# Attention and two feed-forward layers on one core: the first units in halves, means of V in column groups, masks over half the rows

## The chip, the cores and the metric

One core of a Trainium2 chip runs the whole program. The metric is the device time of one execution in microseconds; the median of several runs stands for a kernel, and the profile shows one more execution, recorded instruction by instruction.

## What is computed

The reference chains three parts over 2 batches of 768 tokens (8 heads of 64, so 512 features):

```python
# attention: each query sees keys closer than 16 and one summary per block of 32
k_sum = k.reshape(B, H, nb, 32, D).max(axis=3)
v_sum = v.reshape(B, H, nb, 32, D).mean(axis=3)
scores_l = where(|i - j| < 16, scale * q @ k.T, -1e9)
scores_s = scale * q @ k_sum.T + log(32)
a = softmax(concat(scores_l, scores_s))          # 1e-9 added to the sum
x = a @ concat(v, v_sum)
# two feed-forward layers, 512 -> 2048 -> 512, on all 1536 tokens
h = x @ w_in;  x = (h * cos(h)) @ w_out
h = x @ w_in2; out = (h * clip(h + 3, 0, 6) / 6) @ w_out2
```

## The kernel before

**Attention.** The tokens are cut into 12 units of 128 (6 of each batch). A unit's queries are two windows of 64, and each window needs 96 keys of the band and the 24 block summaries, 120 columns (KC). `load_kt` brings the batch's K transposed, in one piece for each of the four head pairs (HP), into `ktile`; `prep_k` takes the maxima of each block of 32 keys into `ksum` ("key maxima"), and `put_k` copies them into the two buffers `kcat`. `front(u)` does a unit's first half: q is loaded; "masks" writes the additive mask into two PSUM banks (one for each of the heads of a pair) by a matmul of the identity with the mask, 128 rows each, and the sum over keys is added to it; "window" copies the band's keys beside the maxima in `kcat` (for units 0 and 1 one head pair at a time); "scores" are 16 matmuls of 64x64 tiles, each of which shows as two passes in the trace, as all matmuls of 32-bit floats here; then VectorE takes the row maxima ("largest", "negative"), ScalarE the exp with its sums ("power"), VectorE the inverse ("sum", "inverse"), and VectorE or GpSimd scales ("scaled"). `back(u)` transposes the weights on TensorE ("flip"), copies them out of PSUM ("flipped"), multiplies with V ("weighted", line 705) and splits the result into a high and a low part ("x hi", "x lo").

**Means of V.** `prep_v` loads the batch's V in six tiles of 128 rows and multiplies each with an averaging matrix, 32 columns wide, on bank e ("means"). In batch 0 all six go to one column group, rows 96 to 127, where the windows need them; in batch 1 they go to four column groups in turn, which are copied out ("means out"), summed by a matmul with `pick` ("means over") and copied back ("means back"). `put_v` copies the 24 rows of means into both window buffers `vcat`.

**Feed-forward.** Weights come as 64-bit words and are rebuilt as 32-bit floats ("carry", "rebias", "shift", "sign", "join"), then split into a high and a low part ("hi", "lo"). Products with them ("first", line 885; "second", line 1003) take three matmuls each. Twelve steps over 256 tokens of the first layer run beside the attention; a "switch" then hands the attention's memory to the rest, which waits for the whole attention. The later steps form 39 sets of two, each a product of blocks by seven smaller ones ("block product", line 836) whose sums VectorE adds ("add", line 849). A cosine and an exp need different tables on ScalarE, so a change between them costs a table load.

**The order.** Every operation is put into a `Graph` with its dependences, the engines that may run it and a cost. A planner works out due times, adds to them a lead by kind and phase (`LEAD`: a negative number is earlier), simulates the engines once and writes out the order of each engine's queue, SP's with the DMA issues included. There were two phases, before and after the "switch". Where its plan shows gaps on TensorE, it puts dummy matmuls with a tile of zeros (lines 973 and 978); "wake" (line 530) is twelve of these at the start.

Of the kernel before, what the change touches and what calls it, by code (L numbers as in the profile page):

```python
# [22 lines left out]
P = 128  # L23
# [13 lines left out]
class Graph:  # L37
# [22 lines left out]
        "add": (0.0, -116.7), "block product": (0.0, 0.3), "carry": (6.7, 17.2), "cosine": (-4.2, -220.4),  # L60
        "first": (-53.2, -2.5), "flip": (-1.5, 0.0), "g hi": (2.7, 7.6), "g lo": (-6.7, 0.0), "gate": (-0.5, -0.8),
        "gate six": (0.0, 1.0), "half sums": (-0.4, 0.0), "hi": (-143.8, -2.4), "identity": (-9.1, 0.0),
        "inverse": (-7.8, 0.0), "join": (0.0, -0.7), "lo": (-19.9, 0.7), "load k": (-8.7, 0.0), "mask": (-9.8, 0.0),
        "means": (2.6, 0.0), "means back": (4.3, 0.0), "means out": (2.1, 0.0), "means over": (-4.9, 0.0),
        "negative": (-2.5, 0.0), "power": (-1.9, 0.0), "put k": (30.7, 0.0), "rebias": (0.0, 8.2),
        "relu": (0.0, -31.9), "rest": (0.0, -1.8), "scaled": (-1.0, 0.0), "shift": (-11.0, 0.0), "sign": (1.0, 9.0),
        "store": (0.0, -4.8), "sum": (-309.7, 0.0), "switch": (0.0, -6.1), "take": (0.0, -128.3),
        "tees hi": (0.0, -6.8), "turns": (8.0, -1.4), "wake": (7.1, 0.0), "weighted": (6.0, 0.0),
        "weights": (-1.1, -17.2), "window": (-6.2, 0.0), "x lo": (1.4, 0.0), "y hi": (0.0, 5.2),
# [7 lines left out]
    def op(self, kind, engines, fn, r=(), w=(), due=None, table=None, at=0.0, twice=False):  # L77
# [17 lines left out]
        if kind == "switch":  # L95
            self.late = 1
# [95 lines left out]
    def run(self):  # L192
# [12 lines left out]
        due = [d + self.LEAD.get(k, (0.0, 0.0))[late] for d, (k, late) in zip(due, self.kinds)]  # L205
# [39 lines left out]
def attention_two_ffn(  # L245
# [124 lines left out]
    vmean = kv.tile([P, H, D], F32, name="vmean")  # L370
    vcat = ring(kv, "vcat", NKV, [KC, 2, H, D])
# [48 lines left out]
    pick = kv.tile([P, NB], F32, name="pick")  # L420
    nc.gpsimd.memset(pick, 0.0)
    for g in range(P // BLK):
        sl = slice(BLK * g, BLK * g + NB)
        nc.gpsimd.tensor_copy(pick[sl], ident[sl, BLK * g:BLK * g + NB])
# [3 lines left out]
    G.op("identity", {"ACT": act(P)}, lambda e: nc.scalar.copy(ident_r, ident), w=["ident_r"], at=CONST)  # L428
    G.op("mask", {"ACT": act(3 * KC)}, lambda e: nc.scalar.copy(mask_hi, mask), w=["mask_hi"], at=CONST)
# [101 lines left out]

    def load_kt(b):
        for hp in range(HP):
            G.op("load k", {"SP": dma(P * S * 4, 330.0)}, lambda e, hp=hp: nc.sync.dma_start(
                out=ktile[0][:, hp, :], in_=kt[b, :, hp, :]), w=[("kt", hp)])

    def prep_k(b):
        for hp in range(HP):
            G.op("key maxima", {"DVE": dve(S)}, lambda e, hp=hp: nc.vector.tensor_reduce(
                ksum[b][:, hp, :], ktile[0][:, hp, :].rearrange("p (n t) -> p n t", t=BLK), AX.X, ALU.max,  # L540
            ), r=[("kt", hp)], w=[("ks", b, hp)])

    def put_k(b, i):
        n = HP * 2 * NB
        G.op("put k", {"DVE": dve(n, 2), "POOL": one(n)}, lambda e: VEC[e].tensor_copy(
            kcat[i][:, :, :, WK:KC], ksum[b].unsqueeze(2).to_broadcast([P, HP, 2, NB])
        ), r=[("ks", b, hp) for hp in range(HP)], w=[("kcs", i)], twice=True)
# [7 lines left out]
    def prep_v(b):  # L555
# [21 lines left out]
        for ts in [(t,) for t in range(TB)] if b == 0 else (range(NQ4), range(NQ4, TB)):  # L577
            def mean(e, ts=ts):
                for k in ts:
                    g = k % NQ4 if b else NQ4 - 1  # L580
                    nc.tensor.matmul(  # L581
                        bank["e"][BLK * g:BLK * (g + 1)], avg[:, BLK - NS * (k + 1):2 * BLK - NS * (k + 1)],
                        vstage(k)[0], start=k < NQ4 if b else k == 0, stop=k + NQ4 >= TB if b else k == TB - 1,
                        skip_group_check=True)

            G.op("means", {"PE": 1.0 if b else 0.88}, mean,
                 r=[vstage(k)[1] + (h,) for k in ts for h in range(2)] + [
                     vstage(k)[1] for k in ts if k >= NVN], w=["e"])
        if b:
            G.op("means out", {"ACT": act(DM), "DVE": dve(DM)}, lambda e: copy(  # L590
                e, vmean.rearrange("p h d -> p (h d)"), bank["e"]), r=["e"], w=["vm"])
            G.op("means over", {"PE": 0.97}, lambda e: nc.tensor.matmul(
                bank["e"][WK:KC], pick, vmean.rearrange("p h d -> p (h d)"), start=True, stop=True),
                 r=["vm"], w=["e"])
            G.op("means back", {"ACT": act(DM), "DVE": dve(DM)}, lambda e: copy(
                e, vmean[WK:KC], bank["e"][WK:KC].rearrange("p (h d) -> p h d", h=H)), r=["e"], w=["vm"])

    def put_v(b, i):
        src, cost = (vmean[WK:KC].rearrange("n h d -> n (h d)"), dve(2 * DM, 2)) if b else (
            bank["e"][WK:KC], dve(2 * DM))  # L600
        G.op("put v", {"ACT": act(2 * DM), "DVE": cost}, lambda e: copy(
            e, vcat[i][WK:KC].rearrange("n a h d -> n a (h d)"),
            src.unsqueeze(1).to_broadcast([NB, 2, H * D]),
        ), r=["vm"] if b else ["e"], w=[("vcs", i)] + ([] if b else ["e_read"]), twice=bool(b))

    BESIDE = (1, 3)

    def front(u):
# [5 lines left out]
        groups = [(hp, hp + 1) for hp in range(HP)] if first else [(0, HP)]  # L614

        spk = ["a0", "a1"] if u in BESIDE else ["c0", "c1"]
        sp = [bank[n][:, 0:HP * KC] for n in spk]
        m = 0 if tb == 0 else (2 if tb == TB - 1 else 1)
        s4 = [x.rearrange("p (h c) -> p h c", h=HP) for x in sp]

        def masks(e):
            for j in range(2):
                nc.tensor.matmul(
                    sp[j], ident_r, mask_hi[:, m, :].unsqueeze(1).to_broadcast([P, HP, KC]),
                    start=True, stop=False)

        G.op("masks", {"PE": 2 * mm(HP * KC) + 0.08}, masks, r=["mask_hi"], w=spk)

        k, kc = u % NKV, kcat[u % NKV]

        def scores(z0, z1):
            for hp in range(z0, z1):
                for half in range(2):
                    qs = slice(QH * half, QH * half + QH)
                    for j in range(2):
                        nc.tensor.matmul(  # L636
                            s4[j][qs, hp, :], qt[qi][D * j:D * j + D, hp, qs],
                            kc[D * j:D * j + D, hp, half, :], start=False, stop=hp == HP - 1)

        for z0, z1 in groups:  # L640
            keys = bass.AP(
                tensor=ktile[0].tensor, offset=ktile[0][:, z0:z1, a[0]:S].offset,
                ap=[list(ktile[0].ap[0]), [S, z1 - z0], [a[1] - a[0], 2], [1, WK]],
            )
            n = (z1 - z0) * 2 * WK
            G.op("window", {"ACT": act(n), "DVE": dve(n, 2), "POOL": one(n)}, lambda e, z0=z0, z1=z1, keys=keys: copy(
                e, kc[:, z0:z1, :, 0:WK], keys),
                r=[("kt", hp) for hp in range(z0, z1)], w=[("kcw", k, hp) for hp in range(z0, z1)], twice=True)
            G.op("scores", {"PE": 0.98 * (z1 - z0) / HP}, lambda e, z0=z0, z1=z1: scores(z0, z1),
                 r=[("qt", qi), ("kcs", k)] + [("kcw", k, hp) for hp in range(z0, z1)], w=spk)  # L650
        ef = es[ei].rearrange("p j h c -> p (j h) c")
        mx, nmx, sm, sme, rs = (small[n][si] for n in ("mx", "nmx", "sm", "sme", "rs"))
        ek = [("e", ei, 0), ("e", ei, 1)]

        def largest(e):
            for j in range(2):
                nc.vector.tensor_reduce(mx[:, j * HP:(j + 1) * HP], s4[j], AX.X, ALU.max)

        G.op("largest", {"DVE": dve(H * KC) + 0.07}, largest, r=spk, w=[("max", si)])
        G.op("negative", {"DVE": 0.1}, lambda e: nc.vector.tensor_scalar(nmx, mx, -scale, None, ALU.mult),  # L660
             r=[("max", si)], w=[("mx", si)], twice=True)

        def power(e):
            for j in range(2):
                for hp in range(HP):
                    c = j * HP + hp
                    nc.scalar.activation(ef[:, c, :], s4[j][:, hp, :], AF.Exp, bias=nmx[:, c:c + 1], scale=scale,  # L667
                                         accum_out=sm[:, c:c + 1])
# [558 lines left out]
```

## Time and profile before

| | |
|---|---|
| median of 3 runs (lowest, highest) | 591.78 us (590.32, 592.02) |
| profiled execution, its own time | 590.25 us |
| span of the profiled execution | 588.5 us |
| attention ends, later part begins | 107.33 us |
| busy: TensorE, VectorE, ScalarE, GpSimd | 579.1, 497.7, 379.2, 246.1 us |
| read from and written to HBM | 47.71 and 3.15 MB |

The span is what the trace covers; the execution's own time is a little longer. Engines work at the same time, so busy times don't add up.

### The profile page before, as it was taken

What the parts mean: (1) busy time and instruction counts of PE and PEld (TensorE: products, weight loads), DVE (VectorE), ACT (ScalarE), POOL (GpSimd) and SP (SyncE); (2) the same over time, 40 slices, a digit from 0 to 9 for tenths busy, and PEclk for the clock granted to TensorE, in tenths of its full rate; (3) what the DMA queues carried; (4) which work ended last, traced back from release to release, by engine and by line L of the source; (5) the groups of instructions that cost most, each with busy time, mean ns of one, the idle gap of its engine ahead of it and who ended that gap; (6) DMA issues with size and microseconds to landing.
All of it is one profiled execution on the core that took longest, in us unless ns stands there. A gap on an engine that the chain in (4) does not pass through costs nothing.

```text
span 588.5 us, 10756 instructions
## 1 busy us (share of the span) xinstructions
PE 579.1 (98%) x4110; PEld 508.3 (86%) x4110; DVE 497.7 (85%) x913; ACT 379.2 (64%) x798; POOL 246.1 (42%) x230
## 2 busy tenths in 40 slices
PE   9989999899999999999999999999999999999997
PEld 5678789788888989899898898988989889899896
DVE  5999999889999989999999999879968995884554
ACT  4989999676655676776667758567655643553321
POOL 4155565364755553356156553552423351420000
PEclk9999999999999999999999999999999999999999
DMA  8985343201203122320310201232311330200111
GB/s 294 318 297 169 131 138 128 72 1 36 72 36 107 38 72 72 109 72 36 109 37 1 72 26 47 97 116 75 140 40 37 109 107 1 73 0 2 72 73 71
DMA packets 17012, 51.55 MB, mean 88 GB/s; under 512 B 1984, under 2 KB 1984, under 8 KB 16960
## 3 DMA queue, kind: packets, MB, share of 16 engines
q1 hardware_dynamic: 16960, 50.86, 25.0%
q8 instruction: 32, 0.52, 0.4%
q14 instruction: 20, 0.16, 0.1%
HBM read 47.71 MB, written 3.15 MB: 86 GB/s over the span
## 4 chain that ended last, share of the span: by engine, by line
PE 92%; ACT 4%; DMA 2%; DVE 1%; issue 0%; ACTq 0%
PE bank_a L1003 24%; PE bank_d L836 17%; PE bank_b L1003 10%; PE bank_c L1003 10%; PE bank_c L836 8%; PE bank_e L836 8%; PE bank_d L885 5%; PE bank_e L705 1%; PE bank_c L885 1%; PE bank_e L885 1%; PE bank_e L581 1%; ACT es L667 1%; PE bank_c L636 1%; PE bank_b L690 1%; DMA raw<-in_w_out_dram 1%; PE bank_d L530 1%
## 5 line engine op out<-in xcount | busy, mean ns | idle before, releaser
L522 POOL TENSOR_TENSOR cv_y<-cv_t,cv_y 128x512 int32<-128x512 int32 x38 | 52.4, 1380 | 88.0 <-DVE cv_t L520 60.1
L849 DVE TENSOR_TENSOR hs<-bank_d,hs 128x256 f32<-128x256 f32 x100 | 42.1, 422 | 23.0 <-PE bank_d L836 21.6
L957 ACT ACTIVATE ch_c<-hs,three 128x512 f32<-128x512 f32 x48 | 34.3, 723 | 40.1 <-DVE hs L849 39.2
L441 ACT CAST ghi<-ch_c 128x512 fp32r<-128x512 f32 x82 | 50.0, 618 | 14.4 <-DVE ch_c L959 8.4
L963 POOL TENSOR_TENSOR glo<-ch_c,ghi 128x512 fp32r<-128x512 f32 x21 | 28.5, 1363 | 69.5 <-ACT ghi L441 69.4
L520 DVE SCALAR_TENSOR_TENSOR cv_t<-raw,cv_t 128x512 int32<-128x512 int32 x64 | 51.2, 809 | 0.1
L963 DVE TENSOR_TENSOR glo<-ch_c,ghi 128x512 fp32r<-128x512 f32 x63 | 44.1, 713 | 0.8 <-ACT ghi L441 0.2
L503 ACT ACTIVATE cv_y<-raw 128x512 int32<-128x512 uint32 x59 | 39.3, 675 | 2.9 <-DVE wlj_out L458 1.8
L513 ACT ACTIVATE cv_t<-raw 128x512 f32<-128x512 f32 x53 | 35.8, 675 | 7.1 <-DMA raw<-in_w_in_dram 2.7
L458 POOL TENSOR_TENSOR plo<-cv_y,phi 128x512 fp32r<-128x512 f32 (+1 forms) x19 | 22.1, 1163 | 43.4 <-DVE phi L441 26.2
L959 DVE SCALAR_TENSOR_TENSOR ch_c<-ch_c,hs 128x512 f32<-128x512 f32 x48 | 37.0, 780 | 2.1 <-ACT ch_c L957 0.3
L441 ACT COPY hs<-bank_d 128x256 f32<-128x256 f32 x37 | 13.8, 373 | 30.7 <-PE bank_d L836 30.2
L849 DVE TENSOR_TENSOR hs<-bank_c,hs 128x256 f32<-128x256 f32 x48 | 20.3, 423 | 13.4 <-PE bank_c L836 12.6
L836 PE MATMUL bank_d<-xlo,phi 128*128 128x256 f32 x156 | 31.4, 283 | 0.0
L836 PE MATMUL bank_d<-xhi,phi 128*128 128x256 f32 x156 | 31.4, 283 | 0.0
L836 PE MATMUL bank_d<-xhi,plo 128*128 128x256 f32 x156 | 31.4, 282 | 0.0
L518 DVE TENSOR_SCALAR cv_t<-cv_t 128x512 int32<-128x512 int32 x64 | 30.5, 480 | 0.6 <-ACT cv_t L513 0.4
L849 DVE TENSOR_TENSOR hs<-bank_e,hs 128x256 f32<-128x256 f32 x47 | 19.9, 422 | 12.2 <-PE bank_e L836 11.5
L836 PEld LDWEIGHTS bank_d<-xhi,phi 128*128 128x128 f32 x156 | 26.4, 190 | 3.7 <-DVE hs L849 1.0
L948 ACT ACTIVATE ch_c<-hs,quarter 128x512 int32<-128x512 f32 x30 | 21.3, 723 | 12.1 <-DVE hs L849 11.5
L952 ACT ACTIVATE ch_c<-ch_c,half_pi 128x512 f32<-128x512 f32 x37 | 25.9, 717 | 4.9 <-DVE ch_c L950 4.6
L667 ACT ACTIVATE es<-bank_c,nmx 128x120 f32<-128x120 f32 x80 | 27.6, 375 | 0.6 <-DVE nmx L660 0.5
(346 smaller groups left out, 1989.1 us busy)
## 6 DMA issues: line engine op xcount, KB each, us to landing
raw<-in_w_in_dram SPq DMA_DIRECT2D x32, 512.0 KB, 3.4
raw<-in_w_out_dram SPq DMA_DIRECT2D x32, 512.0 KB, 3.2
vcat<-in_vw_dram SPq DMA_DIRECT2D x12, 384.0 KB, 3.9
ktile<-in_kt_dram SPq DMA_DIRECT2D x8, 384.0 KB, 5.0
qt<-in_q_dram SPq DMA_DIRECT2D x12, 256.0 KB, 5.8
out_dram<-total SPq DMA_DIRECT2D x8, 256.0 KB, 2.0
total<-in_vw_dram SPq DMA_DIRECT2D x6, 256.0 KB, 5.6
out_dram<-totak SPq DMA_DIRECT2D x4, 256.0 KB, 2.0
```

Source lines behind the costliest of these rows:

```text
L441: nc.scalar.copy(o, i) if e == "ACT" else VEC[e].tensor_copy(o, i)
L503: nc.scalar.activation(y, low.bitcast(U32), AF.Copy, scale=2.0 ** -29)
L513: nc.scalar.activation(o, a, AF.Copy, scale=2.0 ** -112)
L520: G.op("sign", {"DVE": dve(DM)}, lambda e: nc.vector.scalar_tensor_tensor(t, high, -0x80000000, t, ALU.bitwise_and, ALU.bitwise_or), r=[rk ...
L522: G.op("join", {"POOL": pool(DM), "DVE": dve(DM)}, lambda e: VEC[e].tensor_tensor(y, t, y, ALU.add), r=[tk], w=[yk], twice=True)
L836: nc.tensor.matmul(o, wt[i][:, A[a], kk * P:(kk + 1) * P], xt[:, kk, :], start=first and n + kk == 0, stop=n + kk == 3, skip_group_check=True)
L849: G.op("add", {"DVE": dve(HALF)}, lambda e: nc.vector.tensor_tensor(o[0](), a, b[0](), ALU.add), r=[ak, b[1], "room"], w=[o[1]])
L885: nc.tensor.matmul(h, w["in"][i][:, kk * P:(kk + 1) * P], x[blk][:, kk, c0:c1], start=p + kk == 0, stop=p == 2 and kk == NK - 1)
L957: G.op("relu", {"ACT": act(N) + 0.1}, lambda e: nc.scalar.activation(c(), h(), AF.Relu, bias=three), r=hk, w=ck)
L959: G.op("gate six", {"DVE": dve(N)}, lambda e: nc.vector.scalar_tensor_tensor(c(), c(), 6.0, h(), ALU.min, ALU.mult), r=hk, w=ck, twice=boo ...
L963: G.op("g lo", {"DVE": dve(N), "POOL": pool(N)}, lambda e: VEC[e].tensor_tensor(gbuf("lo", s)[:, 0:N], c(), gh().bitcast(F32), ALU.subtrac ...
L1003: nc.tensor.matmul(acc(s, i)[0], l, r, start=first, stop=end and p == 2 and (N == TOK or i % 2 == 1), skip_group_check=N < TOK)
```

## The change

- Units 0 and 1 are done by halves of two head pairs (`halves`). Each half has banks of its own (c0 and c1, then a0 and a1), masks, scores, maxima, exps, sums and scaling. Their scores read the band from `ktile` and the maxima from `ksum`, two matmuls (96 and 24 columns) in place of one of 120, without the copies into `kcat`. The flips of these units go by halves too.
- In batch 0 the last head pair of K is loaded, and its maxima are taken, in two pieces.
- Each tile's means of V are four matmuls of 128 columns, one for each column group, six operations per batch. They are copied out as 128x128. Batch 0 spreads them by four matmuls with a wider `pick` into rows 96 to 119 of bank e, from where two copies fill the first window and a third, possibly on GpSimd, the second. Batch 1 sends them into all windows by four DMAs ("send v").
- For the inner units (1 to 4 of each batch) the mask's matmuls contract over 64 rows, with `twice`, a doubled identity: rows 0 to 63 for one bank, 64 to 127 for the other.
- `LEAD` has a third phase: units 0 and 1 with the first weights, the rest until the "switch", and after it. All its numbers are new. The wake-up has eleven matmuls.

```diff
     LEAD = {
-        "add": (0.0, -116.7), "block product": (0.0, 0.3), "carry": (6.7, 17.2), "cosine": (-4.2, -220.4),
...
-        "power": (-1.9, 0.0), "put k": (30.7, 0.0), "rebias": (0.0, 8.2),
...
+        "add": (0.0, 0.0, -29.32), "carry": (23.75, 303.3, 627.96), "cosine": (0.0, -80.78, -6.05),
...
+        "power": (0.0, -220.62, 0.0), "put v": (-13.66, 0.0, 0.0), "rebias": (0.0, 3.26, 82.59),
...
         if kind == "switch":
-            self.late = 1
+            self.late = 2
...
+    twice = kv.tile([P, P], F32R, name="twice")
+    both = [ident[:, c:c + QH].unsqueeze(1).to_broadcast([P, 2, QH]) for c in (0, QH)]
...
+    def pieces(b):
+        last = [(HP - 1, c, c + S // 2) for c in (0, S // 2)] if b == 0 else [(HP - 1, 0, S)]
+        return [(hp, 0, S) for hp in range(HP - 1)] + last
...
+        for k in range(TB):
+            def mean(e, k=k):
+                for c in range(NC4):
                     nc.tensor.matmul(
+                        bank["e"][BLK * c:BLK * (c + 1), 0:CC], avg[:, BLK - NS * (k + 1):2 * BLK - NS * (k + 1)],
+                        vstage(k)[0][:, c * CC:(c + 1) * CC], start=k == 0, stop=k == TB - 1)
...
+        G.op("means out", {"ACT": act(CC), "DVE": dve(CC)}, lambda e: copy(e, vmean, bank["e"][:, 0:CC]), r=["e"], w=["vm"])
+        if b == 0:
+
+            def over(e):
+                for c in range(NC4):
+                    nc.tensor.matmul(
+                        bank["e"][WK:KC, c * CC:(c + 1) * CC], pick[:, c * NB:(c + 1) * NB], vmean, start=True, stop=True)
...
+            for c in range(P // BLK):
+                G.op("send v", {"SP": 0.4}, lambda e, c=c: nc.sync.dma_start(
+                    out=vcats.rearrange("k i a h d -> k (i a) (h d)")[WK:KC, :, c * CC:(c + 1) * CC],
+                    in_=vmean[BLK * c:BLK * c + NB].unsqueeze(1).to_broadcast([NB, 2 * NKV, CC])),
...
+    def halves(u):
+
+        return [(0, HP // 2), (HP // 2, HP)] if u < 2 else [(0, HP)]
...
+        for g, (z0, z1) in enumerate(halves(u)):
+            spk = ["a0", "a1"] if u in BESIDE and not first or g else ["c0", "c1"]
...
+                    js = slice(QH * j, QH * (j + 1)) if m == 1 else slice(0, P)
+                    nc.tensor.matmul(
+                        sp[j], (twice if m == 1 else ident_r)[js], mask_hi[js, m, :].unsqueeze(1).to_broadcast(
+                            [js.stop - js.start, nz, KC]), start=True, stop=False)
...
+                            if first:
+                                nc.tensor.matmul(o[:, 0:WK], l, ktile[0][js, hp, a[half]:a[half] + WK], start=False, stop=False)
+                                nc.tensor.matmul(o[:, WK:KC], l, ksum[b][js, hp, :], start=False, stop=last)
+                            else:
+                                nc.tensor.matmul(o, l, kc[js, hp, half, :], start=False, stop=last)
...
+    WAKE = 11
...
+        G.late = 0 if u < 2 else 1
```

## Rows read from the trace of the kernel before

**Rows 1.** Page, part 1: busy time, share of the span, instructions.

```profile
span 588.5 us, 10756 instructions
...
PE 579.1 (98%) x4110; PEld 508.3 (86%) x4110; DVE 497.7 (85%) x913; ACT 379.2 (64%) x798; POOL 246.1 (42%) x230
```

**Rows 2.** Chain of waits in time order: start us, us, what, instructions.

```profile
7.15 2.05 PE bank_d L973 x9
...
12.36 4.41 PE bank_e L581 x10
...
48.38 0.48 PE bank_c L623
...
60.86 1.00 PE bank_e L581 x8
...
62.44 0.98 PE bank_e L581 x4
...
64.77 0.97 PE bank_e L592 x2
65.73 0.63 PE bank_c L623 x2
66.36 0.98 PE bank_c L636 x32
...
71.57 1.08 PE bank_e L705 x32
...
74.72 0.43 PE bank_c L623 x2
...
101.84 1.11 PE bank_e L705 x32
...
107.33 5.74 PE bank_d L885 x24
```

**Rows 3.** Engines' busy us by stretch; then clock, DMA share, GB/s.

```profile
10.00:50.00 40.00, 37.76 (x483) 27.51 (x476) 35.67 (x71) 36.12 (x128) 16.18 (x17) 1.00 0.89 299
50.00:100.00 50.00, 50.00 (x638) 43.24 (x638) 45.24 (x105) 49.24 (x145) 27.01 (x27) 1.00 0.39 129
107.30:350.00 242.70, 242.35 (x1409) 214.50 (x1410) 225.80 (x389) 164.46 (x290) 126.36 (x99) 1.00 0.16 57
```

**Rows 4.** Dummies of line 973 alone: TensorE, weight loads, clock, DMA, GB/s.

```profile
0.00:107.33 107.33, 7.25 (x26) 4.59 (x26) 1.00 0.61 202
```

**Rows 5.** Timeline, 0 to 26 us: start us, us, engine, line, operation, tiles.

```profile
5.09 0.94 DVE L539 TENSOR_REDUCE ksum<-ktile 128x24 f32<-128x768 f32 x1
...
7.15 1.80 DVE L539 TENSOR_REDUCE ksum<-ktile 128x24 f32<-128x768 f32 x2
...
10.37 0.43 SPq L494 DMA_DIRECT2D raw<-in_w_in_dram  x1
10.44 1.22 DVE L657 TENSOR_REDUCE mx<-bank_c 128x4 f32<-128x480 f32 x2 [0.62 <-PE bank_c L636]
...
11.90 0.36 ACT L667 ACTIVATE es<-bank_c,nmx 128x120 f32<-128x120 f32 x1 [0.51 <-DVE nmx L660]
...
17.21 0.29 ACT L667 ACTIVATION_READ_ACCUMULATOR es<-bank_a,nmx 128x1 f32 x1
...
22.84 0.69 DVE L458 TENSOR_TENSOR plo<-cv_y,phi 128x512 fp32r<-128x512 f32 x1
...
25.41 0.71 PE L885 MATMUL bank_d<-xhi,phi 128*128 128x256 f32 x4
```

**Rows 6.** DMA issues until 20 us: size, median us to landing.

```profile
raw<-in_w_in_dram SPq DMA_DIRECT2D x1, 512.0 KB, 6.7
```

**Rows 7.** ScalarE's groups, 0 to 107.33 us: busy us, mean ns | idle before.

```profile
L952 ACT ACT_TABLE_LOAD x6 | 7.7, 1283 | 0.1
...
L441 ACT COPY vcat<-vmean 24x1024 f32<-24x1024 f32 x2 | 2.0, 1042 | 0.0
```

**Rows 8.** TensorE's waits from 107.3 us: total us, times, longest.

```profile
PE bank_e L836 <- DVE hs L441: 0.2, 1, 0.2
```

More of the change, by code (lines that the diff above doesn't have):

```diff
@@ L59 @@
     LEAD = {
-        "add": (0.0, -116.7), "block product": (0.0, 0.3), "carry": (6.7, 17.2), "cosine": (-4.2, -220.4),
[L61 to L69, printed above, removed]
+        "add": (0.0, 0.0, -29.32), "carry": (23.75, 303.3, 627.96), "cosine": (0.0, -80.78, -6.05),
@@ new lines @@
+        "first": (0.0, -17.58, -2.48), "flip": (19.67, 16.5, 0.0), "flipped": (-7.73, -1.42, 0.0),
+        "g hi": (0.0, 9.52, -3.63), "g lo": (0.0, 0.0, 0.44), "gate": (0.0, 3.86, 0.0),
+        "gate six": (0.0, 0.0, -3.75), "half sums": (0.0, -8.47, 0.0), "hi": (16.03, -942.02, 0.0),
+        "identities": (18.61, 0.0, 0.0), "identity": (-2.73, 0.0, 0.0), "inverse": (3.69, -376.89, 0.0),
+        "join": (0.0, -16.27, 0.0), "key maxima": (-49.72, -6.16, 0.0), "largest": (-4.1, 0.0, 0.0),
+        "lo": (3.4, 1.17, -0.01), "load k": (-14.86, 2.66, 0.0), "load q": (-15.65, 2.26, 0.0),
@@ new lines @@
+        "load v": (-0.57, 0.0, 0.0), "load window": (0.0, 15.13, 0.0), "mask": (1.43, 0.0, 0.0),
+        "masks": (5.14, 2.5, 0.0), "means": (0.0, 1.96, 0.0), "means out": (8.98, -3.74, 0.0),
+        "means over": (10.38, 0.0, 0.0), "negative": (-11.74, -442.95, 0.0), "pair sums": (0.0, 0.0, -0.74),
+        "power": (0.0, -220.62, 0.0), "put v": (-13.66, 0.0, 0.0), "rebias": (0.0, 3.26, 82.59),
+        "relu": (0.0, 0.0, 3.24), "rest": (0.0, 0.0, -2.54), "scaled": (7.78, -47.03, 0.0),
+        "scores": (-3.87, -73.6, 0.0), "second": (0.0, 85.58, 0.0), "send v": (0.0, 19.82, 0.0),
@@ new lines @@
+        "shift": (0.0, 0.0, -4.29), "sign": (0.0, 7.4, 9.01), "store": (0.0, 0.0, -32.37), "sums": (0.0, 0.0, 0.59),
+        "switch": (0.0, 0.0, 15.13), "take": (0.0, 0.0, -6.71), "tees": (0.0, 0.0, 0.09),
+        "tees hi": (0.0, 0.0, -23.11), "turns": (0.0, -149.19, 5.63), "wake": (-17.77, 0.0, 0.0),
+        "weighted": (40.56, -19.03, 0.0), "weights": (-35.19, 5.17, 6.27), "window": (0.0, -9.3, 0.0),
+        "x hi": (19.16, -103.2, 0.0), "x lo": (0.0, -22.8, 0.0), "y hi": (0.0, 0.0, -7.53), "y lo": (0.0, 0.0, 1.58),
@@ L204, in run @@
             due[i] = late if own is None else min(late, own)
-        due = [d + self.LEAD.get(k, (0.0, 0.0))[late] for d, (k, late) in zip(due, self.kinds)]
+        due = [d + self.LEAD.get(k, (0.0, 0.0, 0.0))[late] for d, (k, late) in zip(due, self.kinds)]
         _, _, on, order = self.forward(due, succ)
@@ L369, in attention_two_ffn @@
     kcat = ring(kv, "kcat", NKV, [P, HP, 2, KC])
-    vmean = kv.tile([P, H, D], F32, name="vmean")
-    vcat = ring(kv, "vcat", NKV, [KC, 2, H, D])
+    vmean = kv.tile([P, DM // (P // BLK)], F32, name="vmean")
+    vcats = kv.tile([KC, NKV, 2, H, D], F32, name="vcats")
+    vcat = [vcats[:, i] for i in range(NKV)]
     qt = ring(kv, "qt", NQ, [P, HP, P])
@@ L418, in attention_two_ffn @@
     nc.vector.tensor_scalar(here, here, 1.0 / BLK, None, ALU.mult)
-    pick = kv.tile([P, NB], F32, name="pick")
+    pick = kv.tile([P, P // BLK * NB], F32, name="pick")
     nc.gpsimd.memset(pick, 0.0)
@@ L423, in attention_two_ffn @@
         sl = slice(BLK * g, BLK * g + NB)
[L424 removed]
+        nc.gpsimd.tensor_copy(pick[sl, NB * g:NB * (g + 1)], ident[sl, BLK * g:BLK * g + NB])
     ident_r = kv.tile([P, P], F32R, name="ident_r")
@@ L546, in put_k @@
             kcat[i][:, :, :, WK:KC], ksum[b].unsqueeze(2).to_broadcast([P, HP, 2, NB])
-        ), r=[("ks", b, hp) for hp in range(HP)], w=[("kcs", i)], twice=True)
+        ), r=[("ks", b, hp, c0) for hp, c0, _ in pieces(b)], w=[("kcs", i)], twice=True)
     def vstage(t):
@@ L575, in prep_v @@
                 G.op("load v", {"SP": 0.45}, load, w=[key + (half,)])
[L577 to L580, printed above, removed]
+        NC4, CC = P // BLK, DM // (P // BLK)
+        for k in range(TB):
+            def mean(e, k=k):
+                for c in range(NC4):
                     nc.tensor.matmul(
[L582 to L588, printed above, removed]
@@ L589, in prep_v @@
-        if b:
[L590 to L596, printed above, removed]
@@ new lines, in mean @@
+                        vstage(k)[0][:, c * CC:(c + 1) * CC], start=k == 0, stop=k == TB - 1)
+            G.op("means", {"PE": 0.3}, mean, r=[vstage(k)[1] + (h,) for h in range(2)] + (
+                [vstage(k)[1]] if k >= NVN else []), w=["e"])
+        G.op("means out", {"ACT": act(CC), "DVE": dve(CC)}, lambda e: copy(e, vmean, bank["e"][:, 0:CC]), r=["e"], w=["vm"])
[4 more added lines that the diff above has]
+                        bank["e"][WK:KC, c * CC:(c + 1) * CC], pick[:, c * NB:(c + 1) * NB], vmean, start=True, stop=True)
+            G.op("means over", {"PE": 0.95}, over, r=["vm"], w=["e"])
@@ L627, in front @@
-        G.op("masks", {"PE": 2 * mm(HP * KC) + 0.08}, masks, r=["mask_hi"], w=spk)
-        k, kc = u % NKV, kcat[u % NKV]
[L631 to L668, printed above, removed]
-        G.op("power", {"ACT": 2.75}, power, r=[("mx", si)] + spk, w=ek + [("sm", si)], table="exp")
-        G.op("sum", {"DVE": 0.13}, lambda e: nc.vector.tensor_scalar(sme, sm, 1.0e-9, None, ALU.add),
-             r=[("sm", si)], w=[("sme", si)], twice=True)
@@ L713, in back @@
         G.op("weighted", {"PE": 1.1}, weighted,
-             r=[("pts", pi, 0), ("pts", pi, 1), ("vcw", k), ("vcs", k)], w=["e"], due=due)
+             r=[("pts", pi, 0), ("pts", pi, 1), ("vcw", k)] + [
+                 ("vcs", k, c) for c in range(P // BLK + (2 if k == 0 else 0))], w=["e"], due=due)
         blk, o = divmod(u, UPB)
@@ L1084, in attention_two_ffn @@
         v = u - AHEAD
+        G.late = 0 if v < 2 else 1
         if v >= 0:
@@ L1106, in attention_two_ffn @@
         for side in SIDES if n < NW0 else SIDES[:1]:
+            G.late = int(n > 0)
             convert(n, side)
```

121 lines of the change are left out of this document (89 added, 32 removed).

## The prediction

> **What bounds the kernel now.** I read the head of the page first: TensorE is busy for 98% of the span of 588.5 us [rows 1]. That share doesn't tell which stage could be shortened, so I went to the chain of waits in order of time, then to the tables by stretch, and to the timeline only for the start.
>
> The chain [rows 2] has three parts. From 107.33 us to the end it is TensorE alone: the table of 107.3 to 350 us shows 242.35 us of matmuls in 242.7 us [rows 3]. The change removes no work there. From 48.38 to 102.94 us the chain also runs through TensorE without a break, but ScalarE is nearly as full: 49.24 of 50 us between 50 and 100 us [rows 3]. A gain there must relieve both. Before 48.38 us no engine is always last: between 10 and 50 us TensorE is busy for 37.76 us of 40, ScalarE for 36.12, and the DMA engines are at 0.89 of their time with 299 GB/s [rows 3]. TensorE's 7.25 us of dummy matmuls (line 973) before 107.33 us show that its busy time overstates its need [rows 4]. The granted clock is 1.00, the 2.4 GHz level, in every stretch shown [rows 3], so no clock step is to be won.
>
> The late part can't begin before the attention has ended, because its buffers take that memory. So the total is the end of the attention plus some 481 us (588.5 - 107.3) of TensorE work, and the question is by how much 107.33 us moves.
>
> **The start (units 0 and 1 in halves).** Before, the second key maximum ends at 6.03 us, the last at 8.95; then come copies of the maxima, scores, the row maxima (10.44, 1.22 us), and the first exp at 11.90; the exps of both units end at 17.50 (17.21 + 0.29) [rows 5]. That is 5.6 us for four half units, 1.4 each. After, the first half needs two K pieces only. From the dummies' end, 9.20 [rows 2], where the scores begin, to the exp took some 2.6 us; half of the row maxima make it about 2.0, so the first exp is at 6.03 + 2.0 = 8.0 if q is there. The second halves start from 8.95, with no copies of maxima and no window copies ahead: 8.95 + 2.0 = 10.9, while ScalarE works at the first halves until 8.0 + 2.8 = 10.8. All four end at 10.9 + 2.8 = 13.7, which is 3.8 us sooner.
>
> How much of the 3.8 us reaches the first FFN step, at 25.41 us [rows 5]? It needs both units and the first weights. Their load is issued at 10.37 us [rows 5] and takes 6.7 us [rows 6], so it lands at 17.07; the conversion ends at 22.84 + 0.69 = 23.53 [rows 5]. With load and conversion unmoved the step comes at 23.5, 1.9 us sooner; with these moved too, 3.8. I take the middle, **2.9 us**; the bounds are 0 (transfers set the pace) and 3.8.
>
> The rest of the start lies inside this term. The means of batch 0 are twelve passes on one column group, ten of them in 4.41 us [rows 2], so 5.3. In four groups the 48 passes of 128 columns hold 1.5 times the columns of the eight passes of 512 that took 1.00 us for batch 1 [rows 2], so 1.5 us, and spreading them back has the columns of the 0.97 us row, about 1.0: 2.8 us less. But the exps ended only at 17.50 us anyway, after the means (16.77), so this pays only if the exps come sooner. Against it, each of the two units gets 32 more score passes; at 0.98 us for 32 [rows 2] that is 1.0 us each, at worst, and for each more half some five small VectorE instructions of about 0.2 us. The dummies cover the former. The VectorE work has 4.3 us free between 10 and 50 us [rows 3]. Without these covers the start term loses 2 to 3 us, which its lower bound holds. The doubled identity on GpSimd, the wider pick, one more K transfer and one dummy less at the wake-up I take at nothing: dummies fill TensorE until 9.20 us [rows 2]; without that cover it is 0.4 us at most.
>
> **Between 48 and 103 us.** *Inner masks:* eight units, of which 7 to 10 have their masks in this stretch. Two matmuls take 0.43 us [rows 2]. That halves of 64 rows run side by side is seen in the scores: 32 passes of 120 columns in 0.98 us, 31 ns each, while a lone pass of 512 took 0.44 (4.41 / 10), which is 103 ns for 120; so over three ran at once. Best case: 0.21 us less each, 0.85 for four. But the mask that follows an operation of another tile shape takes 0.63 us, the one that follows full-array work 0.43 [rows 2]: a change of shape costs 0.20 us. The new mask is itself of another shape than FFN work, so where it follows that, the 0.2 is lost again. Of the four, two follow full work (0.43) and two don't. I take 0.4 less.
>
> The Trainium skill ("TensorEngine Tiling (Array Packing)", Key Properties) says that changing the tiling mode, not just the tile, drains the engine; the trace agrees, with the 0.63 us against 0.43. By that rule alone four masks would gain nothing, by the tile count alone 0.85 us.
>
> *Means of batch 1:* 1.00 + 0.98 + 0.97 = 2.95 us before [rows 2]; after, 1.5 if the six come in a row (1.45 less); five more gaps of two shape changes each add up to 2.0 (0.55 more). I take 0.9 less. So this stretch gives **1.3 us**, with bounds 2.3 less and 0.6 more.
>
> *ScalarE here* loses the two copies of means into the windows, 2.0 us in all [rows 7], and may get one short copy; so it doesn't bind in TensorE's place. In their stead four transfers on SP's queue wait for the means, at about 64 us; behind them stand loads of q, windows and weights. Weighting of the unit after it is at 71.57 us [rows 2]: 7 us for something that took 6.7 us even in the busiest stretch [rows 6], at 0.39 DMA load. Nothing, then; without that cover each microsecond late costs a microsecond.
>
> **The leads** change no work, only the order. Order could remove the dummies after the first scores, 7.25 - 2.05 = 5.2 us [rows 2, 4], or cost ScalarE a further pair of table loads, 2 x 1.28 = 2.6 us [rows 7]. Exps now go far ahead of cosines in phase 1 (leads -220.6 and -80.8; before -1.9 and -4.2), which can do either. I take **1.0 us** less, a fifth of the dummies, with bounds 2.6 to either side.
>
> **Sum.** 2.9 + 1.3 + 1.0 = 5.2 us. The profiled execution took 590.25 us, so 585.05; the median of the runs, 591.78, stands 1.53 above it, so 586.6 on the median.
>
> **Rivals.**
> *The transfers set the start.* The same bytes must come in, and 0.89 of the DMA time is used already. Only the 1.3 us stay: 590.5. Against it: attention of two units needs little of what moved by 50 us. 13 in 100.
> *Shape changes eat the tiles.* With 0.20 us at every change of shape and other work between all means: masks 0, means 0.55 more, start and leads as forecast, 586.6 + 1.3 + 0.55 = 588.4. For it speaks the 0.63 us against 0.43; against it that the six means share one due time. 10 in 100. (The drain that the Trainium skill's tiling page names would be its mechanism.)
> *More table loads.* Six pairs now, one for two cosines; two more pairs on a ScalarE that is full cost 5.1 us: 591.7. 7 in 100.
> *Slower: the third phase of leads.* The late part has 39 sets of block products, whose sums VectorE must add in time; it is busy for 225.8 of 242.7 us there [rows 3]. The lead of these adds falls from -116.7 to -29.3. One wait of 0.2 us of this kind is there now [rows 8]; if every set had one, 7.8 us: 594.4. It decides from 0.18 us a set, where 586.6 + 7.0 is 0.3% over the median. 8 in 100.
> *More than forecast:* 3.8 + 2.3 + 2.6 = 8.7 us, so 583.1. 10 in 100.
>
> **How the numbers follow.** The forecast itself has 52 in 100, its own range 584 to 588.5. A measurement of this kernel can tell about 0.3%, 1.8 us, from no change. Faster: 52 + 10 + 10 and a fourth of the first rival, 75; same: the rest of that rival and the table loads, 17; slower 8. For 8 in 10 the range reaches from 581.5, a little under the larger gain, to 591.5, near the case of more table loads.
>
> **What would show it.** First exp near 8 us and the exps of units 0 and 1 done near 14; first FFN matmul between 21.6 and 23.5; an inner mask at 0.22 us after tiled work and near 0.43 after full work; no copies of means on ScalarE near 67 us; twelve table loads as now; attention's last unit done near 102 us; from there the same 481 us. The prediction is wrong if ScalarE stands idle after 14 us waiting for q or weights, if table loads grow in number, or if TensorE shows idle time after the attention.

## The result and the profile after

The changed kernel takes 586.27 us (median of four; 586.06 to 586.92), the kernel before 591.64 (also four): a ratio of 0.9915, with a 95% interval of 0.9897 to 0.9933. The forecast was 586.6. The profiled execution took 586.07 us, 4.2 less than that of before. In the experiments the kernel before took 590.8 us (medians of 7 to 29 executions on each chip); against that the gain is 4.5 us rather than 5.4. TensorE's mean granted clock differs between executions (0.986 to 1.000; 1.000 in all four of the changed kernel), and it is named below where a time hangs on it. The total came out as forecast; the way there did not, and most of what follows is about that.

The head of the page of the changed kernel:

```profile
PE 577.8 (99%) x4271; PEld 512.5 (88%) x4271; DVE 497.3 (85%) x918; ACT 377.9 (65%) x796; POOL 250.1 (43%) x232
```

Its chain of waits in order of time, to be held against [rows 2] (start, us, what, instructions):

```profile
13.86 0.79 PE bank_e L601 x24
...
15.24 0.36 PE bank_e L601 x8
...
16.62 0.57 PE bank_e L601 x16
...
18.20 0.98 PE bank_e L612 x8
...
47.44 3.14 PE bank_d L939 x24
...
63.92 1.49 PE bank_e L601 x48
...
71.57 0.41 PE bank_c L663 x2
...
87.13 0.64 PE bank_c L663 x2
...
101.52 1.23 PE bank_e L758 x32
102.75 1.27 PE bank_a L1057 x9
104.02 5.47 PE bank_d L939 x24
```

The attention ends at 104.02 us, not 107.33: 3.3 us of the gain lie before this point, 0.9 behind it (480.28 us to the end, where before it was 481.17). The means of batch 1 are one piece of 1.49 us, 63.92 to 65.41, in place of 2.95 in three. Inner masks take 0.41 to 0.42 us whatever stands ahead of them; the mask of unit 11, still over 128 rows and behind a weighting, takes 0.64. At the end, 1.27 us of feed-forward work (line 1057) stands behind the last weighting (101.52).

The start, in the timeline, to be held against [rows 5]:

```profile
0.74 0.39 SPq L507 DMA_DIRECT2D raw<-in_w_in_dram  x1
...
1.18 1.36 SPq L554 DMA_DIRECT2D ktile<-in_kt_dram  x3
...
4.83 0.68 SPq L507 DMA_DIRECT2D raw<-in_w_out_dram  x1
...
7.56 2.27 DVE L559 TENSOR_REDUCE ksum<-ktile 128x24 f32<-128x768 f32 x3
...
8.69 0.42 PE L677 MATMUL bank_c<-ktile,qt 64*64 64x96 f32 x8
...
9.74 0.71 DVE L704 TENSOR_REDUCE mx<-bank_c 128x2 f32<-128x240 f32 x2
...
10.38 0.54 DVE L559 TENSOR_REDUCE ksum<-ktile 128x12 f32<-128x384 f32 x1
...
11.23 0.36 ACT L713 ACTIVATE es<-bank_c,nmx 128x120 f32<-128x120 f32 x1
...
19.56 0.22 ACT L713 ACTIVATION_READ_ACCUMULATOR es<-bank_a,nmx 128x1 f32 x1
...
29.53 0.74 PE L939 MATMUL bank_d<-xhi,phi 128*128 128x256 f32 x4
```

The first weights go out ahead of K (0.74 us), the second ahead of V (4.83). The last maxima of K end at 10.92 us (10.38 + 0.54) instead of 8.95. The first half's scores begin at 8.69, but VectorE takes their row maxima only at 9.74, after maxima of further pieces of K, and the last piece's maxima stand between them and the first exp. That exp is at 11.23 instead of 11.90, the exps of units 0 and 1 end at 19.78 instead of 17.50, and the first FFN matmul comes at 29.53 instead of 25.41. But for the first exp the start is later, not sooner.

Busy times by stretch of the changed kernel (TensorE, weight loads, VectorE, ScalarE, GpSimd; then clock, DMA share, GB/s), to be held against [rows 3]:

```profile
10.00:50.00 40.00, 38.97 (x590) 30.93 (x589) 35.70 (x86) 38.17 (x136) 20.32 (x22) 1.00 0.93 305
50.00:100.00 50.00, 49.92 (x713) 45.44 (x712) 44.83 (x102) 48.00 (x142) 27.49 (x26) 1.00 0.41 137
...
100.00:110.00 10.00, 9.74 (x78) 8.46 (x78) 9.33 (x15) 6.78 (x12) 3.25 (x4) 1.00 0.22 68
...
104.02:584.30 480.28, 476.29 (x2863) 425.56 (x2861) 408.03 (x717) 285.56 (x510) 194.49 (x153) 1.00 0.18 62
```

and two stretches of the kernel before that were not shown:

```profile
100.00:110.00 10.00, 8.23 (x100) 6.88 (x99) 7.95 (x16) 5.62 (x13) 0.87 (x1) 1.00 0.16 55
...
107.33:588.50 481.17, 476.95 (x2864) 425.94 (x2864) 406.49 (x716) 285.87 (x508) 196.53 (x156) 1.00 0.18 62
```

TensorE's idle time around the attention's end (100 to 110 us) fell from 1.77 us to 0.26. ScalarE has 48.00 us to do between 50 and 100 us, not 49.24. The dummies of line 973, now 1027, grew from 7.25 us [rows 4] to 10.59:

```profile
0.00:104.02 104.02, 10.59 (x36) 6.21 (x36) 1.00 0.63 211
```

Where the 3.3 us before the attention's end lie, TensorE's busy time from 48 us to this end shows, first all of it, then the dummies alone (the tile of zeros); the changed kernel, then the kernel before:

```profile
48.00:104.02 56.02, 55.68 (x781) 1.00 0.39 129
48.00:104.02 56.02, 1.36 (x8) 1.00 0.39 129
...
48.00:107.33 59.33, 57.48 (x760) 1.00 0.38 126
48.00:107.33 59.33, 0.08 (x1) 1.00 0.38 126
```

All of the 3.3 us lie here (56.02 for 59.33). Work other than dummies is 3.1 us less (54.32 for 57.40), idle time 1.5 less (0.34 for 1.85), and dummies are 1.3 more. Of the 3.1 us, 1.5 are the means of batch 1 and 0.5 the masks of units 7 to 10 (0.67, 0.63, 0.43 and 0.43 us before); the other 1.1 us is, by difference, work that TensorE had already done by 48 us, unit 6's scores among it. That point itself is uncertain by some 0.7 us: in the kernel with dummies for batch 1, below, the row at 47.44 us stands at 48.11, although nothing ahead of it was changed.

In the later part the one wait for VectorE's sums is as long as it was [rows 8]:

```profile
PE bank_c L890 <- DVE hs L903: 0.2, 1, 0.2
```

### The profile page after: what moved, and what is told of

Its sections match the earlier page's. It is cut to its first block, busy times and chain, and to the rows that moved or that the text cites. A ratio compares the mean times of both kernels' runs of the same rounds, so it can differ in the third digit from the quotient of the medians.

```text
span 584.3 us, 11086 instructions
## 1 busy us (share of the span) xinstructions
PE 577.8 (99%) x4271; PEld 512.5 (88%) x4271; DVE 497.3 (85%) x918; ACT 377.9 (65%) x796; POOL 250.1 (43%) x232
## 4 chain that ended last, share of the span: by engine, by line
PE 88%; DVE 6%; ACT 2%; DMA 2%; issue 1%; SPq 0%; ACTq 0%; DVEq 0%
PE bank_a L1057 22%; PE bank_d L890 16%; PE bank_b L1057 10%; PE bank_c L1057 10%; PE bank_c L890 8%; PE bank_e L890 7%; PE bank_d L939 5%; PE bank_b L743 1%; PE bank_e L758 1%; PE bank_e L939 1%; PE bank_c L939 1%; DMA raw<-in_w_in_dram 1%; PE bank_c L680 1%; PE bank_d L1027 1%; ACT es L713 1%; PE bank_d L543 1%
## 5 line engine op out<-in xcount | busy, mean ns | idle before, releaser
L535 POOL TENSOR_TENSOR cv_y<-cv_t,cv_y 128x512 int32<-128x512 int32 x34 | 46.5, 1368 | 77.4 <-DVE cv_t L533 56.0
L1017 POOL TENSOR_TENSOR glo<-ch_c,ghi 128x512 fp32r<-128x512 f32 x23 | 31.3, 1369 | 73.8 <-ACT ghi L454 73.7
L533 DVE SCALAR_TENSOR_TENSOR cv_t<-raw,cv_t 128x512 int32<-128x512 int32 x64 | 49.1, 776 | 0.1
L1017 DVE TENSOR_TENSOR glo<-ch_c,ghi 128x512 fp32r<-128x512 f32 x61 | 45.3, 751 | 1.1 <-ACT ghi L454 0.7
L1013 DVE SCALAR_TENSOR_TENSOR ch_c<-ch_c,hs 128x512 f32<-128x512 f32 x48 | 38.2, 807 | 1.9 <-ACT ch_c L1011 0.3
L531 DVE TENSOR_SCALAR cv_t<-cv_t 128x512 int32<-128x512 int32 x64 | 35.1, 556 | 1.6 <-ACT cv_t L526 1.5
```

The source lines that it names most:

```text
L531: G.op("shift", {"DVE": dve(DM, 2)}, lambda e: nc.vector.tensor_scalar(t, t, 3, None, ALU.logical_shift_left), w=[tk], twice=True)
L533: G.op("sign", {"DVE": dve(DM)}, lambda e: nc.vector.scalar_tensor_tensor(t, high, -0x80000000, t, ALU.bitwise_and, ALU.bitwise_or), r=[rk ...
L535: G.op("join", {"POOL": pool(DM), "DVE": dve(DM)}, lambda e: VEC[e].tensor_tensor(y, t, y, ALU.add), r=[tk], w=[yk], twice=True)
L1013: G.op("gate six", {"DVE": dve(N)}, lambda e: nc.vector.scalar_tensor_tensor(c(), c(), 6.0, h(), ALU.min, ALU.mult), r=hk, w=ck, twice=boo ...
L1017: G.op("g lo", {"DVE": dve(N), "POOL": pool(N)}, lambda e: VEC[e].tensor_tensor(gbuf("lo", s)[:, 0:N], c(), gh().bitcast(F32), ALU.subtrac ...
```

## The experiments

All ratios are to the kernel before on the same chip (its median there was about 590.8 us); a ratio need not equal that of the two medians. Differences to the changed kernel are to its 586.27 us above. The planner works out a new order as soon as a cost, a lead or the graph changes; in four kernels (masks, the two with dummies, short means) it doesn't, since the planner's costs were left as they are.

### Same order: masks over 128 rows

```diff
-                    js = slice(QH * j, QH * (j + 1)) if m == 1 else slice(0, P)
+                    js = slice(0, P)
...
-                        sp[j], (twice if m == 1 else ident_r)[js], mask_hi[js, m, :]...
+                        sp[j], ident_r[js], mask_hi[js, m, :]...
```

> The changed kernel with all masks over 128 rows, in the same order of instructions on every engine. If only the tile count mattered, each of the eight inner units loses 0.21 us: 1.7 us, 588.0 us, of which 0.85 us after 48 us. If a change of shape costs 0.2 us each time, only masks that follow tiled work lose: 0.4 to 0.8 us in all, 586.7 to 587.1 us. If neither is on the path: 586.3 us.

586.61 us, ratio 0.9909 (0.9875 to 0.9944): the same as the changed kernel within its interval. The masks of units 7 to 10 in its chain:

```profile
52.86 0.44 PE bank_c L663 x2
...
63.01 0.44 PE bank_c L663 x2
...
72.75 0.63 PE bank_c L663 x2
...
81.46 0.43 PE bank_c L663 x2
```

Three of the four follow full-array work and take 0.43 to 0.44 us; over half the rows they took 0.41 to 0.42. Only the third follows a weighting, and there 0.63 became 0.41. So the four are worth 0.3 us together in this order. The time can't tell the second expectation from the third; the rows speak for the second. The tiles do run side by side (in the timelines two matmuls over 64 rows take 0.48 to 0.49 us together, two over 128 rows, of this run, 0.60 to 0.70), but the change of shape takes the gain back wherever there was none before.

### Same order: dummies in the place of the means saved

```diff
 # dummies behind the spreading of batch 0's means
+                fill(13)
 # dummies behind the last means of batch 1 (another kernel)
+                if b and k == TB - 1:
+                    fill(7)
```

> The changed kernel with thirteen dummy matmuls of 0.215 us, 2.8 us, behind the matmuls that spread the means of batch 0 (near 19 us), so that TensorE has there what the change took away; the order is the same. If the gain of the means in batch 0 is on the path: 589.0 us. If the start has that much room on TensorE: 586.3 to 587 us.

589.12 us, ratio 0.9960 (0.9942 to 0.9978): 2.8 us more than the changed kernel by the medians, about the length of the dummies. TensorE's timeline:

```profile
19.63 3.47 PE L1028 MATMUL bank_d<-zero 128*128 128x512 f32 x14
22.94 0.60 PE L744 MATMUL bank_b<-ident,es 128*120 128x128 f32 x4
...
27.35 1.89 PE L1028 MATMUL bank_d<-zero 128*128 128x512 f32 x7
...
33.10 0.74 PE L940 MATMUL bank_d<-xhi,phi 128*128 128x256 f32 x4 [0.24 <-DVE xhi L454]
```

The thirteen dummies and one of the planner's (line 1028) run from 19.63 us, and the flips that stood at 19.45 us follow them, at 22.94. The first FFN matmul moves from 29.53 to 33.10; 0.5 us of this stood before the dummies already. The masks and scores of units 2 and 3 wait behind the dummies too. Between them and the first FFN matmul stand ten dummies of the planner's, seven of them at 27.35 us. They are part of the fixed order and run whether TensorE has time or not, so the room that they fill can't take up the new work. The run shows that work added to this order costs its length. That the 2.6 us saved on the means were worth as much isn't shown by it: the planner, which fills gaps with dummies, might have left some of these out.

> The changed kernel with seven dummy steps of two matmuls of 256 columns, 1.5 us, behind the last means of batch 1 (near 65 us), what the change took away there; the order is the same. If TensorE sets the pace of this stretch: 587.7 to 588 us, the 1.5 us in full. If ScalarE does (48.0 of 50 us busy): 586.3 to 587 us.

588.03 us, ratio 0.9942 (0.9914 to 0.9970): 1.8 us more by the medians. The intervals of the two ratios overlap, but no execution of either kernel falls among the other's (587.78 to 589.04 here). In the profiled executions the same operations run 0.67 us late ahead of the dummies and 2.05 behind them (75 us), 1.4 us for 1.5 us of dummies. In this stretch TensorE sets the pace; ScalarE, less loaded than before, does not.

### Same order, kernel before: fewer means in batch 0

```diff
                 for k in ts:
+                    if b == 0 and k in (1, 2, 3):
+                        continue
```

> The kernel before with three of the six matmuls that make batch 0's means of V left out (its summaries of V are wrong by that), in the same order: TensorE has 2.6 us less to do between 12.4 and 16.8 us. If TensorE's work in the start is on the path: 588.0 to 588.5 us. If the start waits for exps and transfers, as my prediction had it: 590 to 591 us, no change.

589.70 us, ratio 0.9993 (0.9973 to 1.0014): no change that can be told by the ratio, and the 2.6 us in full are ruled out. But the twelve executions fall into two groups. Seven with a mean granted clock of 0.999 or 1.000 took 589.00 to 589.81 us, where 23 such executions of the kernel before have a median of 590.70; five with 0.993 to 0.997 took 590.72 to 593.49. So at the full clock about 1.4 of the 2.6 us reach the end (the median of the seven is 589.32), and a lower clock in five of twelve executions (0.997 or less in four of 29 before) takes them back in the mean. Two of the short kernel's waits between 10 and 60 us (total, times, longest) show where the rest is lost; in the kernel before the first is not there and the second is 0.5 us:

```profile
PE bank_b L692 <- DVE es L677: 1.0, 1, 1.0
PE bank_c L638 <- DMA qt<-in_q_dram: 1.0, 1, 1.0
```

### New order: the leads

```diff
 # old_leads: the changed kernel with
+    LEAD = the kernel before's, its first phase for both phases until the switch
 # new_leads: the kernel before with
+    LEAD = the changed kernel's, and its three phases
```

> The changed kernel, ordered with the leads of the kernel before (first phase's numbers for units 0 and 1 and for the rest until the switch). If the gain of 5.4 us is less work on TensorE (masks, means), most of it stays: 586 to 588 us. If it comes from the new order, in which the attention runs ahead of the feed-forward steps and the last of these covers the attention's end, it goes: 590 to 593 us. My prediction gave the leads 1.0 us: 587.3.

600.52 us, ratio 1.0181 (1.0126 to 1.0235).

> The kernel before, ordered with the new leads in three phases, and nothing else. If the order is worth the gain by itself: 587 to 588 us. If the gain is less work on TensorE: 590 to 592 us. Since these leads were found for another graph, a time above 592 us says only that they don't fit, and nothing on where the gain came from.

602.10 us, ratio 1.0182 (1.0147 to 1.0217). Leads fit the graph for which they were found and lose some 14 and 11 us on another. A part of this is the clock: in the one execution of each whose mean granted clock was 1.000 the two took 598.26 and 598.48 us, still 12 us over the changed kernel and 8 over the kernel before, and in the profiled ones (0.986 and 0.991) the clock stood at 0.50 for about ten us around the attention's end. Neither run prices a part, so the leads were searched anew for the graph in question, by the end that the planner itself works out:

```diff
 # before_leads3: the graph before, three phases, leads of its own
+    LEAD = searched anew
 # after_leads2: the changed graph, units 0 and 1 with the rest of the attention
+    LEAD = searched anew, first phase = second phase
```

> The kernel before, its graph unchanged, with leads in three phases searched anew for it (by the planner's own end, as the planner of the kernel works them out). The earlier run with the changed kernel's leads said only that leads fit one graph. If less work on TensorE is the whole gain: 590 to 591 us. If the order carries as much as the work: 587.5 to 589 us. My prediction's 1.0 us for the leads would be 590.6 less 1.0: 589.8.

589.92 us, ratio 0.9980 (0.9962 to 0.9998): 1.2 us from the order alone, on the old graph (0.1 to 2.2 by the interval; 0.8 by the medians).

> The changed kernel with two phases of leads (units 0 and 1 with the rest of the attention), searched anew for it. If two phases are enough for what the change does: 586 to 586.8 us. If a phase of its own for the start is worth a good part: 588 to 589 us.

595.77 us, ratio 1.0078 (1.0053 to 1.0103), worse than the kernel before. In its trace the later part begins at 113.17 us, 9 us later than in the changed kernel; until 125 us TensorE waits 1.9 us for high parts of x, 1.1 and 0.6 us for loads of V, and 0.7 to 0.9 us each for several results of VectorE. Its clock isn't the cause: executions with 0.999 took 592.90 and 595.74 us. A search that ends in an order with such waits prices no phase.

### New order: units 0 and 1 whole

```diff
-        return [(0, HP // 2), (HP // 2, HP)] if u < 2 else [(0, HP)]
+        return [(0, HP)]
```

> The changed kernel with units 0 and 1 done whole (banks c0 and c1, a0 and a1 as before), their scores still from the K tile. If the halves bring the start forward and the start sets the end (my prediction's 2.9 us): 588.5 to 589.5 us. If the start is set by the first weights and by what follows the exps: 586 to 587 us, within 0.3% of the changed kernel.

595.25 us, ratio 1.0079 (1.0064 to 1.0095), with leads that were found for halves. With leads of its own:

> The changed kernel with units 0 and 1 done whole, as in the earlier run, but with leads searched anew for this graph in the same way. If the halves are worth the 2.9 us of my prediction's start term: 589 us. If they are worth nothing beside a fitting order: 586 to 586.8 us.

592.43 us, ratio 1.0020 (1.0002 to 1.0038), 6 us over the changed kernel, although the planner put both ends at the same time. Two of TensorE's waits until 110 us (total, times, longest) and busy times in stretches of 2 us:

```profile
PE bank_e L643 <- DMA total<-in_vw_dram: 1.2, 2, 1.1
PE bank_e L643 <- DMA vnat<-in_vw_dram: 1.2, 1, 1.2
```

```profile
14.00:16.00 2.00, 0.67 (x13) 0.20 (x15) 1.93 (x7) 2.00 (x14) 0.00 (x0) 1.00 0.93 338
16.00:18.00 2.00, 0.93 (x16) 0.32 (x16) 1.96 (x4) 2.00 (x14) 0.00 (x0) 0.76 0.89 319
18.00:20.00 2.00, 2.00 (x32) 1.55 (x32) 0.00 (x0) 0.27 (x2) 0.00 (x0) 0.50 0.90 352
...
22.00:24.00 2.00, 2.00 (x12) 1.33 (x10) 1.56 (x4) 1.30 (x4) 0.00 (x0) 0.54 1.01 368
```

The means of V wait 2.4 us for loads; TensorE is busy for 0.67 and 0.93 of 2 us, and then its granted clock is 0.50, the 1.2 GHz level, until near 24 us. The planner has neither in its plan: gaps that it sees it fills with dummies. The clock is only a part of the 6 us: the three of twelve executions with 0.999 or 1.000 took 589.55 to 590.60 us, still 3.3 to 4.3 over the changed kernel and near the 589 us of the expectation in which the halves are worth 2.9. But the waits for V belong to this order, so the run doesn't price the halves by themselves.

### New order: K ahead of the first weights

```diff
-        "weights": (-35.19, 5.17, 6.27)
+        "weights": (0.0, 5.17, 6.27)
```

> The changed kernel with the lead of the first weights' load at 0 in place of -35.19, so that K and q are asked for before them. The first exp should come near 9 us, in place of 11.2. If an early attention start is what counts, the time falls to 584 to 586 us. If the early conversion of the first weights counts as much, it stays at 586 to 587 us or rises to 589.

593.43 us, ratio 1.0044 (1.0027 to 1.0061). The first scores and the first exp, and ScalarE's loads of the cosine's table until 130 us, here and then in the changed kernel:

```profile
8.05 0.42 PE L677 MATMUL bank_c<-ktile,qt 64*64 64x96 f32 x8 [1.38 <-DMA qt<-in_q_dram]
...
11.09 0.36 ACT L713 ACTIVATE es<-bank_c,nmx 128x120 f32<-128x120 f32 x1 [1.31 <-DVE nmx L707]
```

```profile
L1006 ACT ACT_TABLE_LOAD x8 | 10.3, 1283 | 0.1
```

```profile
L1006 ACT ACT_TABLE_LOAD x7 | 9.0, 1283 | 0.1
```

With K first, the first exp is at 11.09 us, hardly sooner than 11.23: the scores wait 1.38 us for q, whose load stands in the same stream. The first FFN matmul does come sooner (26.40), but the attention ends at 110.03 us: the planner's new order has one more pair of table loads, 2.6 us on ScalarE, and at the attention's end TensorE is busy for 8.20 us of 10 (100 to 110 us). An early first FFN step alone doesn't make the kernel fast.

### New order: batch 1's means by copies

```diff
-        if b == 0:
+        if True:
...
-        if b:
+        if False:
```

> The changed kernel with the means of batch 1 spread by matmuls and copied into the windows, as those of batch 0, in place of the four transfers. TensorE gets 1.0 us more, ScalarE or others up to 2 us; the wait of the weighting for the transfers (0.3 us) goes. If TensorE sets the pace: 587 to 587.5 us. If the transfers, which hold up SP's queue for 4 us, cost as much as they save: 586.3 us. If ScalarE sets the pace: 588 us or more.

593.50 us, ratio 1.0044 (1.0016 to 1.0072): only the open range for ScalarE (588 us or more) holds it. The order changed at the end of the attention. Two rows of TensorE's timeline there, and stretches of 2 us:

```profile
97.36 1.15 PE L758 MATMUL bank_e<-pts,vcats 120*64 120x64 f32 x32
...
103.51 1.97 PE L758 MATMUL bank_e<-pts,vcats 120*64 120x64 f32 x30 [1.92 <-ACT pts L454]
```

```profile
104.00:106.00 2.00, 2.00 (x29) 1.88 (x28) 1.63 (x3) 0.52 (x2) 0.00 (x0) 0.50 0.03 8
...
116.00:118.00 2.00, 2.00 (x8) 1.55 (x8) 0.07 (x1) 0.79 (x2) 0.83 (x1) 0.71 0.55 217
```

All feed-forward steps of the first part are done by 100.5 us, so nothing covers the attention's last chain; TensorE waits 1.92 us for a copy by ScalarE, the granted clock falls to 0.50 and stays there until about 117 us, and 30 passes of the weighting take 1.97 us, where 32 took 1.15. This execution is the slowest of ten (598.53 us). The four with a mean granted clock of 1.000 took 591.64 to 593.89, so the clock doesn't explain why the kernel is still 5 to 8 us slower than the changed one at the full clock. The uncovered end fits that; no run tests it. What the four transfers are worth by themselves is not settled by this run.

## Why the prediction was right, point by point

**What bounds the kernel** held: the later part is TensorE's alone, 480.3 us after, 481.2 before, and 3.3 of the 4.2 us between the profiled executions come from the attention's end. The slower rival (late sums) did not come; the wait is 0.2 us as before.

**The start, 2.9 us: wrong, and the step that failed.** I let K and q come as early as before and the first weights unmoved. The leads, which I took for a mere order with 1.0 us, put the loads of the first weights ahead of K and of V, and the step that was to come at 21.6 to 23.5 us came at 29.53. Even with K first, the first exp is at 11.1, not 8.0, since the scores wait for q (my "if q is there") and VectorE takes the row maxima only at 9.76 us. No time is gained by 48 us; at most 1.1 us came out of the start, as work done ahead of that point. The rival that the transfers set the start was nearer here, at 13 in 100, though VectorE's order held the first exp too; it had the total wrong, because more came from elsewhere. My remark that the means of batch 0 pay only if the exps come sooner held by half in the kernel before: with three of six left out, some 1.4 of 2.6 us came through at the full clock. In the changed kernel 2.6 us are saved on these means (5.3 before; 0.79, 0.36, 0.57 and 0.98 now), while the dummies of line 1027 are 3.3 us more. What the saving is worth there stays open: 2.8 us of work put into its place cost 2.8 in an order whose dummies couldn't give way.

**Between 48 and 103 us, 1.3 us: right, with one size off.** The means of batch 1 gave 1.46 us (forecast 0.9), since all six stand in a row. The masks gave 0.3 in the same order (forecast 0.4) and 0.5 between the two profiles, where three of the four now stand behind full-array work. My sign for them was wrong: a mask over half the rows was to take 0.22 us after tiled work, and it takes 0.41 there too, because the change of shape that was in the 0.63 us stays. The Trainium skill ("TensorEngine Tiling (Array Packing)", Key Properties) says that changing the tiling mode drains the engine. The runs agree: 0.43 became 0.41 us behind full work, where the change is new, and 0.63 became 0.41 behind a weighting, where it was there before. That TensorE sets the pace there, and ScalarE doesn't take its place, the dummies showed (1.5 us of them cost 1.4 in the profile, 1.8 by the medians).

**The four transfers at nothing: nearly.** They were issued from 65.76 us on, one by one over 4 us, and the weighting of unit 6, at 70.12 us, waited for them: its 32 passes took 1.45 us in place of 1.15.

```profile
65.76 3.97 SPq L623 DMA_DIRECT2D vcats<-vmean  x4
...
70.12 1.45 PE L758 MATMUL bank_e<-pts,vcats 120*64 120x64 f32 x32
```

The 7 us of cover that I counted had shrunk to 4.7 (from the end of the means at 65.41), since the weighting came sooner.

**The leads, 1.0 us: not to be told apart from the start.** The 4.2 us between the profiled executions are 2.0 less work on the means of batch 1 and the masks, 1.1 of work done ahead of 48 us, 1.5 of idle time that is gone, mostly at the attention's end, where feed-forward work now covers it, less 1.3 of dummies, and 0.9 in the later part, where two dummies of 0.62 us are gone. These are differences of rows; that a piece is worth its full length is shown for the means of batch 1 alone. Idle time, dummies and the later part together are 1.1, close to my 1.0; with the work done ahead, which may be the order's or the halves', it would be 2.2. The covered end fits exps that go far ahead of cosines. Table loads did not grow: thirteen on lines 713 and 1006 until 130 us, as many as before. A new order alone gave 1.2 us on the graph before.

So the errors met, which is luck: at least 1.8 us too many for the start, against 0.7 too few for the stretch from 48 to 103 us and a little too few for the order. The sum of 5.2 us was 1.0 too large for the profiled executions, and of before that one was among its faster ones (590.25 us against medians of 590.8 to 591.64), while that of the changed kernel is near its median. What the halves are worth stays open. Both runs without them have orders that lose time elsewhere; an order for whole units that keeps TensorE as busy wasn't found.

## What to carry to other kernels

Where the order of a static queue was found by a search, an edit's price and the order's price can't be read from one run: first change the work under an unchanged order (shorter work under the old cost, dummies in the place of what was saved), and only then the order. Dummies that are already in such an order don't give way to new work, so see first whether any stand behind the place. Time saved on an in-order engine is worth its length where that engine sets the pace (the means of batch 1), and less where it waits for something else next (in the kernel before, half for the means of batch 0). Compare executions of the same granted clock before a difference is put down to the edit. Where a kernel has a stage that ends in a chain of small steps, independent work kept for its end may cover it; here this fits two traces and was not tested by itself.

## What the runs showed of the hardware

In one execution of the kernel with copies TensorE's granted clock fell from 1.00 to 0.50, the 1.2 GHz level, at 103.5 us, after the engine had stood idle for 1.9 us, and came back only near 117 us; there 30 passes of a weighting took 1.97 us at the lower level, and 32 took 1.15 at the higher. In the kernel with whole units and its own leads it fell at about 17 us, after the waits for V, and came back near 24 us. A planner that doesn't know this prices such gaps at their length alone. It isn't the same in every execution of a kernel: the ten of the kernel with copies had mean granted clocks from 0.987 to 1.000, and the twelve of the kernel with fewer means took 589.0 to 589.8 us at 0.999 or 1.000 and 590.7 to 593.5 at 0.993 to 0.997.
